# Reordering the first loads, and their PSUM banks, of an attention and feed-forward kernel

## The chip, the core and the metric

The kernel runs on one NeuronCore of a Trainium2 chip. The core has a tensor engine (PE, with its weight loads shown apart as PEld), a vector engine (DVE), an activation engine (ACT), a general engine (POOL) and a queue engine (SP), each with an instruction stream of its own; 16 DMA engines move data between HBM and the core's SBUF. PE writes into PSUM, eight banks of 128 partitions x 512 fp32. The metric is the device time of one execution in microseconds.

## The reference

Two parts, one after the other. First attention over a sliding window of 128 with a linear position bias (ALiBi): batch 8, 8 heads, sequence 576, head size 64. Then a feed-forward part over the 4608 tokens with an activation x * cos(x):

```
scores = q @ k.T / sqrt(64);  rel = pos_q - pos_k
scores = where(0 <= rel < 128, scores - slope[h] * |rel|, -1e9)
attn   = softmax(scores) @ v                     # (8, 8, 576, 64)
x      = attn.transpose(0, 2, 1, 3).reshape(4608, 512)
h      = x @ w_in                                # w_in  512 x 2048
out    = (h * cos(h)) @ w_out                    # w_out 2048 x 512
```

Inputs and output are fp32; the kernel computes its products in bf16.

## The kernel before

**Attention.** A batch's 576 queries are cut into blocks of 128 (the last has 64), and a block into units `(batch, block, half of the heads)`: the first and the last block are one unit each, blocks 1 to 3 two each, eight units per batch. A unit goes through: `scores` (products of k and q into two PSUM banks; for the first six units of batch 0 the bias is added by PE, by a product with the identity matrix, L583, ahead of the scores), `exps` (one exponential on ACT over both banks, L596), `mask` (a product on DVE with the exponential of the bias, L615, for all units whose bias was not added by PE), `pv` (product with V, whose 65th column gives the sum, L631 to L645), `norm` (reciprocal and scaling on DVE), and a transposition of the result into `xT`, by PE (`x_pe`) or by a DMA (`x_dma`). Which pair of banks a unit's scores use comes from `SLOT`: slot 0 is banks 4 and 5, slot 1 is 6 and 7, slot 2 is 2 and 3. Before the change the first seven units (phase -1) go in groups of two through slots 0 and 1, and their products with V into banks 2 and 3.

**Feed-forward.** Tokens go in nine chunks of 512. For each of 16 slices of 128 columns of w_in, `moe1` makes four matmuls (512 wide, L760), a sine on ACT (L765) and a product on DVE (L769); then `moe2` makes 64 matmuls with w_out (L813) for the chunk. In chunk 0 the first half of the slices is cut into narrower parts (`moe1_part`, L784), so that they can start as soon as some of the tokens are there. The units of later batches are worked between the matmuls of the chunks. ACT needs a table load to go from exponentials to sines and back.

**Loads.** q and k of batch 0 come in four pieces (`load_qk`, PIECES): piece 0 by SP and ACT, pieces 1 to 3 by POOL's queue; piece 2 ("the third piece", tokens 256 to 511) is the largest, piece 3 (qend, kend) the last 64 tokens. Then batch 1 in one piece each, into the same buffers `qB` as the pieces of batch 0, so that these loads wait until PE has transposed batch 0 out of them. V comes in five blocks of tokens per batch (`load_v`, L392), w_in in four parts (L424), w_out in four quarters (L431). All of these are issued by POOL in the order of the program. q and k are transposed by PE for batches 0 and 1 (`qk_transposes`, L510) and by DMA for the later ones.

**The order of the work.** The program lists operations with what they read and write; class `Plan` sorts them. It keeps a clock per engine, gives every operation an expected duration (`occ`) and an expected time until its result is there (`lat`), and takes, engine by engine, the operation that can start first, then by priority (`pri`) and by place in the list. For a load, `lat` is the time that the transfer keeps the DMA engines busy, summed up in the variable `wire`. POOL keeps the order of the list. The result is one fixed stream of instructions per engine, with waits on semaphores where one engine needs another's result: an engine does not pass a waiting instruction. So constants such as `lat` change no computation, but they change where in the stream each instruction stands. While PE has nothing to do at the start, the planner puts small matmuls on zeros (`filler`, L945) into its stream.

Of the kernel before, what the change touches and what calls it, by code (L numbers as in the profile page):

```python
# [286 lines left out]
def bass_alibi_sliding__then__act_gcu_kernel(  # L287
# [8 lines left out]
    with ExitStack() as ctx:  # L296
# [4 lines left out]
        op = R.op  # L301
# [34 lines left out]

        GROUPS = [[2] * 4] + [[3, 3, 2]] * 5 + [[3] * 3]
        SLOT = [4, 6, 2]
        QUOTA = [8, 8, 8, 8, 8, 8, 9]
        BIASED = [(0, 0, 0)] + [(0, qb, hh) for qb in range(1, 4) for hh in range(2)][:5]  # L340
        SB, UB, OB = [4, 5, 6, 7], [2, 3], [0, 1]
# [24 lines left out]
        def load_qk(which, src, b, n=0):  # L366
            t0, rr, _ = PIECES[b][n]
            c0 = 64 * (t0 // 32)
            rows = bass.AP(src.tensor, src[b].offset + 64 * t0,
                           [[64 * rr, 32], [64 * S, H], [1, 64 * rr]])  # L370
            if b == 0 and n == 0:
                op("sp" if which == "q" else "act", [lambda e: e.dma_start(qF[which][:, :, :], rows)],
                   w=[("qF", which)], dma=f"ld{which}f", occ=700 if which == "q" else 2000,
                   lat=4000 if which == "q" else 3300, pri=0)
                i = qF[which][:, :, :].rearrange("p y (j d) -> p y j d", j=4)
                o = qC[which][:, :, :, :].rearrange("p j y d -> p y j d")
                op(("act", "dve"),
                   {"act": lambda e: e.activation(o, i, ACTF.Copy),
                    "dve": lambda e: e.tensor_copy(o, i)},
                   r=[("qF", which)], w=piece_keys(which, b, n), occ={"act": 460, "dve": 330},  # L380
                   lat={"act": 560, "dve": 410}, pri=2)
                return
            o = qE[which][:, :, :] if t0 == 512 else qB[which][:, :, c0:c0 + 64 * rr]
            op("pool", [lambda e: e.dma_start(o, rows)],  # L384
               w=piece_keys(which, b, n), dma=f"ld{which}{n}", occ=750,
               lat={2: 600, 4: 800 if which == 'q' else 900,
                    8: 2600 if which == 'q' else 1300, 18: 2850}[rr])

        def load_v(b, order=range(NBLK), behind=()):
            for t in order:  # L390
# [32 lines left out]
        def load_w_in(f0, f1):  # L423
            op("pool", [lambda e: e.dma_start(  # L424
                w_in[:, :, 256 * f0:256 * f1],
                moe_w_in[:, 256 * f0:256 * f1].rearrange("(k p) c -> p k c", p=128))],
               w=[("wi", f) for f in range(f0, f1)], dma=f"wi{f0}", occ=750,
               lat=1300 * (f1 - f0))

        def load_w_out(u):  # L430
            op("pool", [lambda e: e.dma_start(  # L431
                w_out[:, 4 * u:4 * u + 4, :],
                moe_w_out[512 * u:512 * u + 512, :].rearrange("(f p) j -> p f j", p=128))],
               w=[("wo", u)], dma=f"wo{u}", occ=750, lat=2600)

        def constants():
            op("dve", lambda e: e.memset(zeros[:, :], 0.0), w=["zeros"], occ=60, pri=0)
# [109 lines left out]
        def t_first(u):  # L547
            return S * u[0] + 128 * u[1]

        def scores(us, slot):  # L550

            def f(e):
                ins = None
                for n, u in enumerate(us, slot):
                    b, qb, hh = u
                    banks = [SLOT[n], SLOT[n] + 1]
                    acc = u in BIASED
                    if qb == 0:
                        jobs = [(128 * pr, 128, pr, 0) for pr in range(NPAIR)]
                    elif qb == 4:  # L560
                        jobs = [(128 * pr + 64 * i, 64, pr, 3 + i) for pr in range(NPAIR)
                                for i in range(2)]
                    else:
                        jobs = [(256 * i + 128 * j, 128, 2 * hh + i, qb - 1 + j)
                                for i in range(2) for j in range(2)]
                    for n, (c0, n_, pr, kc) in enumerate(jobs):
                        stop = not acc or n == len(jobs) - 1
                        for x in range(2):
                            ins = e.matmul(ps[:, banks[x], c0:c0 + n_], keys_ap(b, x, pr, kc),  # L569
                                           query_ap(b, x, pr, qb, n_), start=not acc, stop=stop)  # L570
                return ins
            keys, held, occ = [], [], 0
            for n, u in enumerate(us, slot):
                keys += tkeys(u)
                held += [("B", SLOT[n] + x) for x in range(2)]
                occ += 250 if u[1] == 4 else 230
                if u in BIASED:
                    b, qb, hh = u
                    for x in range(2):
                        rhs = BT[:, x, :, 128:256] if qb == 0 else BT[:, x, 2 * hh:2 * hh + 2, :]  # L580
                        prs = range(NPAIR) if qb == 0 else range(2 * hh, 2 * hh + 2)
                        bank = SLOT[n] + x
                        op("pe", lambda e, rhs=rhs, bank=bank: e.matmul(  # L583
                            ps[:, bank, :], ident[:, :], rhs, start=True, stop=False),
                           r=[("BT", 2 * pr + x) for pr in prs] + ["ident"], w=[("B", bank)],
                           occ=216, lat=379, pri=2)
            op("pe", f, r=keys, w=held, occ=occ, lat=occ + 165, mode=1, pri=2)

        pcount = [0]
        pbuf = {}  # L590
# [1 line left out]
        def exps(u, n, table):  # L592
            banks = [SLOT[n], SLOT[n] + 1]
            i = pbuf[u] = pcount[0] % NP
# [235 lines left out]

        def attention(us, phase):

            begin, g = [], 0
            sizes = ([[2] * 4] + GROUPS + [[], []])[phase + 1]
            own = 3 in sizes
            for many in sizes:
                some = us[g:g + many]
                if phase < 0:
                    for n, u in enumerate(some):
                        scores([u], n)  # L840
                        exps(u, n, 0)
                        mask(u)
                        if us.index(u) == 1:
                            qk_transposes(0, "q", 2, [0], SB[2:4])
                else:
                    scores(some, 0)
                    for n, u in enumerate(some):
                        exps(u, n, 2 * phase + 2)
                if not own:
                    outs = [UB[0] if u[1] in (0, 4) else UB[n] for n, u in enumerate(some)]  # L850
                    for u in some if phase >= 0 else []:
                        mask(u)
                    sets = [list(zip(some, outs))]
                    if phase < 0 or any(u[1] in (0, 4) for u in some):
                        sets = [[x] for x in sets[0]]
                else:
                    sets = [[x] for x in zip(some, SLOT)]
                for set_ in sets:
                    if own:
                        mask(set_[0][0])  # L860
                    pv(set_)
                    after = []
                    for u, ub in set_:
                        n = ucount[0]
                        ucount[0] += 1
                        norm(u, ub, n)
                        soon = us.index(u) < (4 if phase else 2) and phase >= 0
                        after.append((soon, t_first(u) // CH > phase + 1, u, ub, n))
                    for soon, late, u, ub, n in after:
                        if soon:  # L870
                            begin.append(x_dma(u, n))
                        elif late:
                            x_dma(u, n)
                        else:
                            x_pe(u, ub, n)
                g += many
            return begin
# [3 lines left out]
        constants()  # L881
        load_qk("q", q, 0, 1)
        load_qk("k", k, 0, 1)
        load_v(0, [0])
        load_qk("q", q, 0, 2)
        load_qk("k", k, 0, 2)
        load_v(0, [1])
        load_w_in(0, 1)
        load_v(0, [2, 3])
        load_w_in(1, 2)  # L890
# [5 lines left out]
        for n in range(2):  # L896
            qk_transposes(0, "q", n, [0], OB[0:1])
            qk_transposes(0, "k", n, [0], OB[1:2])
        qk_transposes(0, "k", 2, [0], OB)
        every = [u for b in range(B) for u in units(b)]  # L900
        done = 7
        attention(every[0:done], -1)
# [9 lines left out]
        for c in range(NCH):  # L912
# [17 lines left out]
            n = QUOTA[c] if c < len(QUOTA) else 0  # L930
            begin = attention(every[done:done + n], c)
# [4 lines left out]
            while next_t < B and done >= 8 * (next_t - 1):  # L936
# [4 lines left out]
                if next_t < B:  # L941
# [2 lines left out]
            moe2(c)  # L944
        R.schedule(filler=lambda e: e.matmul(ps[:, UB[1], 0:128], zeros[:, :],  # L945
                                             zeros[:, :], start=True, stop=True),
                   fill=(900, 8300))
        R.emit(final=[f"st{i}" for i in range(NOB)])


# [26 lines left out]
```

## Time and profile before

| | us |
|---|---|
| median of 3 runs | 309.34 (309.11 to 309.6) |
| profiled execution | 309.74 |
| its span | 307.9 |
| PE busy | 299.7 |
| ACT busy | 199.9 |
| DVE busy | 194.1 |
| POOL busy | 97.0 |

The span runs from the first to the last instruction; 1.84 us of the profiled execution lie around it. Busy time is what an engine spends in instructions, so an engine's idle time is span less busy time. In a timeline a row gives start, duration, engine, line, operation, tiles and number of instructions, and in brackets the idle time in front of it with what ended it. The digits by slices are busy shares in tenths, each slice a fortieth of the span.

### The profile page before, as it was taken

The numbers are of one execution on the slowest core, as the hardware profiler recorded it, in microseconds if no ns is written. First come the engines' busy times: TensorE is split into PE (matmuls) and PEld (weight loads), VectorE is DVE, ScalarE is ACT, GpSimd is POOL, SyncE is SP. The second block draws the span as 40 slices with busy tenths as digits, with TensorE's granted clock in tenths as the row PEclk, the third lists the DMA queues.
The fourth block names the chain that finished last, engine by engine and source line by source line (L and its number), as shares of the span: only waits on it lengthen the run. The fifth ranks groups of instructions, "written<-read, shape, count | busy, mean of one in ns | idle before, by whom it ended". The sixth has DMA issues, their size and how long they took to land.

```text
span 307.9 us, 6411 instructions
## 1 busy us (share of the span) xinstructions
PE 299.7 (97%) x2556; PEld 157.4 (51%) x2600; DVE 194.1 (63%) x402; ACT 199.9 (65%) x268; POOL 97.0 (32%) x122
## 2 busy tenths in 40 slices
PE   8899999999999999999999999999999999999996
PEld 6685555445554555445544554455445554444444
DVE  6687777574668566856785568656966588742000
ACT  6888854885488746873688378746964588752211
POOL 8997201355055505550348023900500000000000
PEclk9999999999999999999999999999999999999999
DMA  9999999999399979999699959995991420001112
GB/s 148 173 204 207 207 162 203 140 162 181 105 127 130 170 122 141 129 168 106 155 122 156 151 109 150 165 179 96 169 106 44 113 70 0 0 0 70 68 73 97
DMA packets 150332, 39.08 MB, mean 127 GB/s; under 512 B 138912, under 2 KB 145312, under 8 KB 150304
## 3 DMA queue, kind: packets, MB, share of 16 engines
q0 software_dynamic: 100688, 18.10, 80.6%
q1 hardware_dynamic: 49344, 20.33, 33.2%
q8 instruction: 20, 0.33, 0.5%
q10 hardware_dynamic: 272, 0.26, 0.3%
q14 instruction: 8, 0.07, 0.1%
HBM read 36.70 MB, written 9.44 MB: 150 GB/s over the span
## 4 chain that ended last, share of the span: by engine, by line
PE 83%; DMA 7%; POOL 5%; ACT 2%; issue 1%; DVE 1%; POOLq 0%; ACTq 0%
PE ps L813 37%; PE ps L760 36%; DMA w_outb<-in_moe_w_out_dram 7%; PE ps L569 5%; ACT p L596 2%; PE ps L643 2%; PE ps L645 2%; POOL vp L392 1%; PE ps L631 1%; POOL w_inb L424 1%; POOL qrows L384 1%; POOL krows L384 1%; PE ps L635 1%; DVE p L615 1%; POOL w_outb L431 0%
## 5 line engine op out<-in xcount | busy, mean ns | idle before, releaser
L813 PE MATMUL ps<-w_outb,gT 128*128 128x512 bf16 (+2 forms) x566 | 132.8, 373 | 2.6 <-issue 1.1
L760 PE MATMUL ps<-xT,w_inb 128*128 128x512 bf16 x528 | 120.9, 379 | 0.9 <-issue 0.2
L769 DVE TENSOR_TENSOR gT<-ps,cos 128x512 bf16<-128x512 f32 x136 | 90.3, 688 | 21.1 <-ACT cos L765 16.3
L765 ACT ACTIVATE cos<-ps,halfpi 128x512 f32<-128x512 f32 x136 | 90.0, 688 | 18.9 <-PE ps L760 13.9
L596 ACT ACTIVATE p<-ps 128x1024 bf16<-128x1024 f32 x64 | 61.7, 1023 | 33.3 <-PE ps L569 33.3
L760 PEld LDWEIGHTS ps<-xT,w_inb 128*128 128x128 bf16 x544 | 52.0, 98 | 59.5 <-ACT p L596 0.6
L813 PEld LDWEIGHTS ps<-w_outb,gT 128*128 128x128 bf16 x592 | 53.2, 98 | 56.4 <-DMA w_outb<-in_moe_w_out_dram 1.7
L392 POOL DMA_DIRECT2D vp<-in_v_dram x40 | 33.7, 867 | 88.4 <-DMA xT<-xnat 68.9
L615 DVE TENSOR_TENSOR p<-p,emask 128x1024 bf16<-128x1024 bf16 x58 | 39.1, 682 | 26.8 <-ACT p L596 26.7
L820 ACT ACTIVATE ob<-ps 128x512 f32<-128x512 f32 (+2 forms) x21 | 12.1, 576 | 41.8 <-PE ps L813 35.3
L403 POOL DMA_DIRECT2D qnat<-in_q_dram x30 | 25.3, 876 | 23.1 <-DMA qt<-qnat 23.1
L403 POOL DMA_DIRECT2D knat<-in_k_dram x30 | 25.3, 874 | 11.1 <-DMA kt<-knat 8.3
L682 DVE TENSOR_TENSOR xnat<-ps,rec 128x256 bf16<-128x256 f32 x48 | 19.8, 420 | 1.3
L821 DVE COPY ob<-ps 128x512 f32<-128x512 f32 x16 | 10.9, 683 | 15.1 <-PE ps L813 15.1
L569 PE MATMUL ps<-qt,kt 64*128 64x128 bf16 (+1 forms) x576 | 19.4, 211 | 0.4 <-DVE qt L526 0.2
L569 PEld LDWEIGHTS ps<-qt,kt 64*128 64x128 bf16 x576 | 14.5, 94 | 9.7 <-issue 4.5
L643 PEld LDWEIGHTS ps<-vp,p 128*128 128x128 bf16 x192 | 14.2, 97 | 9.0 <-issue 6.1
L643 PE MATMUL ps<-vp,p 128*128 128x65 bf16 x192 | 17.4, 193 | 0.2 <-ACT xT L731 0.2
L645 PE MATMUL ps<-vp,p 128*128 128x65 bf16 x192 | 17.5, 193 | 0.0
L645 PEld LDWEIGHTS ps<-vp,p 128*128 128x128 bf16 x192 | 13.2, 97 | 2.3
L680 DVE RECIPROCAL rec<-ps 128x4 f32<-128x4 f32 x48 | 8.2, 176 | 6.3 <-PE ps L645 5.8
L631 PEld LDWEIGHTS ps<-vp,p 128*128 128x128 bf16 x128 | 7.3, 97 | 3.6 <-issue 1.8
(66 smaller groups left out, 150.0 us busy)
## 6 DMA issues: line engine op xcount, KB each, us to landing
out_dram<-ob SPq DMA_DIRECT2D x35, 256.0 KB, 2.2
vp<-in_v_dram POOLq DMA_DIRECT2D x32, 128.0 KB, 7.1
qnat<-in_q_dram POOLq DMA_DIRECT2D x24, 128.0 KB, 6.6
knat<-in_k_dram POOLq DMA_DIRECT2D x24, 128.0 KB, 5.1
w_outb<-in_moe_w_out_dram POOLq DMA_DIRECT2D x4, 512.0 KB, 21.9
w_inb<-in_moe_w_in_dram POOLq DMA_DIRECT2D x3, 512.0 KB, 12.8
qrows<-in_q_dram POOLq DMA_DIRECT2D x1, 576.0 KB, 15.6
krows<-in_k_dram POOLq DMA_DIRECT2D x1, 576.0 KB, 17.7
```

The lines of the kernel that those rows point to most:

```text
L392: op("pool", [lambda e, t=t, rows=rows: e.dma_start(vp[b % 2][0:rows, t, :, 0:64], v[b, :, 128 * t:128 * t + rows, :].rearrange("h p d -> ...
L403: fns.append(lambda e, t=t, rows=rows: e.dma_start(nat[which][0:rows, t, :, :], src[b, :, 128 * t:128 * t + rows, :].rearrange("h p d -> p ...
L569: ins = e.matmul(ps[:, banks[x], c0:c0 + n_], keys_ap(b, x, pr, kc), query_ap(b, x, pr, qb, n_), start=not acc, stop=stop)
L596: op("act", lambda e: e.activation(P[i][:, 0:1024], ps[:, banks[0]:banks[0] + 2, :].rearrange("p a b -> p (a b)"), ACTF.Exp, scale=0.125), ...
L615: op("dve", lambda e: e.tensor_tensor(p, p, m, ALU.mult), r=[("P", i), ("EM", 0), ("EM", 1)], w=[("P", i)], occ=600, lat=690, pri=1)
L643: e.matmul(o, P[i][:, c0:c0 + 128], V[:, qb - 1, h, 0:65], start=True, stop=False)
L645: ins = e.matmul(o, P[i][:, c0 + 128:c0 + 256], V[:, qb, h, 0:65], start=False, stop=True)
L682: op("dve", lambda e: e.tensor_tensor(o, U[:, :, :, 0:64], rv[:, :, :, None].broadcast_to([128, 2, 2, 64]), ALU.mult), r=[("rec", n % 4)], ...
L760: op("pe", lambda e, kc=kc: e.matmul(ps[:, bank, :], w_in[:, kc, 128 * fc:128 * fc + 128], xT[:, kc, r0:r0 + CH], start=(kc == 0), stop=(k ...
L765: op("act", lambda e: e.activation(cosb[ci][:, :], ps[:, bank, :], ACTF.Sin, bias=halfpi[:, 0:1]), r=["halfpi"], w=[("B", bank), ("cos", c ...
L769: op("dve", lambda e: e.tensor_tensor(gT[gi][:, fc, :], ps[:, bank, :], cosb[ci][:, :], ALU.mult), r=[("cos", ci)], w=[("B", bank)] + [("g ...
L813: op("pe", lambda e, t=t, fc=fc, bank=bank, j0=j0, j1=j1: e.matmul(ps[:, bank, 0:j1 - j0], gT[gi][:, fc, 128 * t:128 * t + 128], w_out[:, ...
```

## The change

V's first block goes behind the third pieces of q and k on POOL's queue, right in front of V's second block. Units 0 to 6 take their score banks from a list `FIRST` (slots 0, 1, 2, 0, 1, 0, 1), and their products with V go to the banks in `FIRST_PV` (0, 0, 2, 2, 3, 2, 3). The bias products of units 1 to 5 are listed as after the scores of unit 0. k's third piece is transposed after unit 2's scores, into banks 2 and 3, no longer ahead of all units into banks 0 and 1. Five of the planner's expected transfer times are lower, and the fillers end at 7.4 us of the planner's clock in place of 8.3. The planner makes all orders anew from this; `mask` itself is not edited, and its products move only as the planner moves them.

```diff
+        FIRST, FIRST_PV = [0, 1, 2, 0, 1, 0, 1], [0, 0, 2, 2, 3, 2, 3]
...
-               lat={2: 600, 4: 800 if which == 'q' else 900,
-                    8: 2600 if which == 'q' else 1300, 18: 2850}[rr])
+               lat={2: 370, 4: 800 if which == 'q' else 900,
+                    8: 1700 if which == 'q' else 1300, 18: 2790}[rr])
...
-               lat=1300 * (f1 - f0))
+               lat=1275 * (f1 - f0))
...
-               w=[("wo", u)], dma=f"wo{u}", occ=750, lat=2600)
+               w=[("wo", u)], dma=f"wo{u}", occ=750, lat=2540)
...
-        def scores(us, slot):
+        def scores(us, slot, after=()):
...
-                           occ=216, lat=379, pri=2)
-            op("pe", f, r=keys, w=held, occ=occ, lat=occ + 165, mode=1, pri=2)
+                           occ=216, lat=379, pri=2, after=after)
+            return op("pe", f, r=keys, w=held, occ=occ, lat=occ + 165, mode=1, pri=2)
...
-                    for n, u in enumerate(some):
-                        scores([u], n)
-                        exps(u, n, 0)
+                    for u in some:
+                        i = us.index(u)
+                        made.append(scores([u], FIRST[i], made[:1]))
+                        exps(u, FIRST[i], 0)
                         mask(u)
-                        if us.index(u) == 1:
+                        if i == 1:
                             qk_transposes(0, "q", 2, [0], SB[2:4])
+                        if i == 2:
+                            qk_transposes(0, "k", 2, [0], UB)
...
-                    outs = [UB[0] if u[1] in (0, 4) else UB[n] for n, u in enumerate(some)]
+                    outs = FIRST_PV[g:g + many] if phase < 0 else [UB[0] if u[1] in (0, 4) else UB[n] for n, u in enumerate(some)]
...
-        load_v(0, [0])
         load_qk("q", q, 0, 2)
         load_qk("k", k, 0, 2)
-        load_v(0, [1])
+        load_v(0, [0, 1])
...
-        qk_transposes(0, "k", 2, [0], OB)
...
-                   fill=(900, 8300))
+                   fill=(900, 7400))
```

In the streams as planned, PE's fillers go from 32 to 34 instructions; POOL has V's first block two places later; before the transposes of batch 1's q PE has 9 of the 512-wide matmuls of chunk 0 in place of 16, between those and the transposes of k 11 in place of 9, and behind these 12 in place of 7.

More of the change, by code (lines that the diff above doesn't have):

```diff
@@ L831, in attention @@
         def attention(us, phase):
-            begin, g = [], 0
+            begin, made, g = [], [], 0
             sizes = ([[2] * 4] + GROUPS + [[], []])[phase + 1]
```

## The prediction

> **What bounds the kernel now.** I read the page first, then the waits of the tensor engine (PE) in order of time, then busy time by stretches, then the DMA issues with their times to landing. The page:
>
> ```profile
> span 307.9 us, 6411 instructions
> PE 299.7 (97%) x2556; PEld 157.4 (51%) x2600; DVE 194.1 (63%) x402; ACT 199.9 (65%) x268; POOL 97.0 (32%) x122
> DMA  9999999999399979999699959995991420001112
> PE 83%; DMA 7%; POOL 5%; ACT 2%; issue 1%; DVE 1%; POOLq 0%; ACTq 0%
> q8 instruction: 20, 0.33, 0.5%
> ```
>
> PE is busy for 97% of the span, so only its 8.2 us of idle time or its order can give anything. The chain of waits starts on POOL, which issues the loads, and goes through the landing of w_out before PE takes it over. The DMA digits say that the 16 DMA engines are full from the first slices to about 90 us. So the edit, which lies within the first 50 us, must be read against landings. The timeline of PE's weight loads, which stand right in front of their matmuls, shows where it waits for them:
>
> ```profile
> 23.30 0.14 PEld L510 LDWEIGHTS ps<-ident,qend 128*64 128x64 bf16 x4 [0.22 <-DMA kend<-in_k_dram]
> ...
> 28.60 1.03 PEld L510 LDWEIGHTS ps<-ident,qrows 128*64 128x64 bf16 x36 [0.51 <-DMA qrows<-in_q_dram]
> ...
> 31.77 1.05 PEld L510 LDWEIGHTS ps<-ident,krows 128*64 128x64 bf16 x36 [0.42 <-DMA krows<-in_k_dram]
> ...
> 34.36 1.47 PEld L813 LDWEIGHTS ps<-w_outb,gT 128*128 128x128 bf16 x8 [0.25 <-DMA w_outb<-in_moe_w_out_dram]
> ...
> 39.44 0.55 PEld L813 LDWEIGHTS ps<-w_outb,gT 128*128 128x128 bf16 x4 [1.05 <-DMA w_outb<-in_moe_w_out_dram]
> ...
> 42.15 0.55 PEld L813 LDWEIGHTS ps<-w_outb,gT 128*128 128x128 bf16 x4 [0.36 <-DMA w_outb<-in_moe_w_out_dram]
> ```
>
> Six times between 23 and 42 us PE stands in front of a transfer: the last pieces of batch 0, q of batch 1, k of batch 1, then w_out's quarters. What PE saves before 23 us, it waits away here. By stretches (the bracketed number is instructions, the last three columns clock, DMA share, GB/s):
>
> ```profile
> 28.60:36.00 7.40, 7.19 (x94) 4.25 (x96) 6.70 (x11) 6.23 (x11) 2.04 (x3) 1.00 1.29 203
> 36.00:39.50 3.50, 2.85 (x35) 1.24 (x34) 1.57 (x4) 2.79 (x3) 0.00 (x0) 1.00 1.29 204
> 39.50:44.00 4.50, 4.34 (x60) 2.49 (x63) 2.66 (x8) 1.94 (x2) 0.00 (x0) 1.00 2.35 159
> 44.00:60.00 16.00, 15.84 (x149) 8.60 (x147) 10.96 (x28) 10.84 (x16) 4.19 (x5) 1.00 1.99 172
> 60.00:300.00 240.00, 237.52 (x1846) 118.42 (x1879) 152.08 (x300) 154.06 (x204) 62.98 (x75) 1.00 1.08 114
> ```
>
> From q's landing at 28.6 to 39.5 us PE idles 0.21 + 0.65 = 0.86 us. From 44 to 60 us it idles only 0.16 us, and over the 240 us after that 2.5 us, spread out: from w_out on, PE has no stall of any size left.
>
> **The change, step by step.** Three things move: the order of loads, the order of work on the start's banks, and, since the planner orders everything anew from its constants, PE's order up to 50 us.
>
> *The loads.* q's and k's third pieces go ahead of V's first block on POOL's queue. The same bytes are loaded and the same instructions issued. The issues and the matching landings:
>
> ```profile
> 2.20 0.72 POOL L384 DMA_DIRECT2D krows<-in_k_dram  x1
> 2.92 0.94 POOL L392 DMA_DIRECT2D vp<-in_v_dram  x1
> 3.85 0.70 POOL L384 DMA_DIRECT2D qrows<-in_q_dram  x1
> 4.54 0.72 POOL L384 DMA_DIRECT2D krows<-in_k_dram  x1
> ...
> 11.52 0.71 POOL L384 DMA_DIRECT2D kend<-in_k_dram  x1
> ...
> 12.98 0.70 POOL L384 DMA_DIRECT2D qrows<-in_q_dram  x1
> ```
> ```profile
> krows<-in_k_dram POOLq DMA_DIRECT2D x1, 128.0 KB, 3.9
> vp<-in_v_dram POOLq DMA_DIRECT2D x1, 128.0 KB, 4.1
> qrows<-in_q_dram POOLq DMA_DIRECT2D x1, 256.0 KB, 5.9
> krows<-in_k_dram POOLq DMA_DIRECT2D x1, 256.0 KB, 6.5
> ...
> kend<-in_k_dram POOLq DMA_DIRECT2D x1, 64.0 KB, 11.7
> ...
> qrows<-in_q_dram POOLq DMA_DIRECT2D x1, 576.0 KB, 15.6
> ```
>
> Issue plus time to landing gives k's second piece at 6.1 us, V's first block at 7.0, q's third piece at 9.75, k's third at 11.0, kend at 23.2, q of batch 1 at 28.6. The third pieces have equal size, yet q's needs 2.73 us behind V's block and k's 1.29 us behind q's: 1.44 us of excess that bytes do not explain. Two bounds for what the new order does to every later landing, as a shift s: if the excess belongs to the piece itself, s = 0; if it belongs to its place behind V's block, s = 1.44. A landing can also come later, since nothing excludes that V's block now takes up such an excess and adds to it; I put the lower end at -0.3. POOL does not set it: it issues q of batch 1 at 12.98 us, 15.6 us before it lands. That issue waits until PE has transposed the third pieces out of the same buffer; those transposes stay ahead of 12.5 us (below), so this stays hidden.
>
> The planner's constants in the diff go the same way: 900 ns less for q's third piece, 2 x 230 for the last pieces, 200 for eight w_in columns, 60 for q of batch 1: it plans with s = 1.62. That is a belief of the code, not a measurement, and I use it only as a neighbour of the upper bound.
>
> *Banks of the start.* Units 0, 1, 2 get pairs 4-5, 6-7, 2-3, so unit 2's scores need not wait for unit 0's exponential.
>
> ```profile
> 8.16 1.97 ACT L596 ACTIVATE p<-ps 128x1024 bf16<-128x1024 f32 x2
> 10.54 1.02 ACT L596 ACTIVATE p<-ps 128x1024 bf16<-128x1024 f32 x1 [0.40 <-PE ps L569]
> ...
> 13.70 2.11 ACT L596 ACTIVATE p<-ps 128x1024 bf16<-128x1024 f32 x2 [0.89 <-PE ps L569]
> 16.12 1.94 ACT L596 ACTIVATE p<-ps 128x1024 bf16<-128x1024 f32 x2 [0.31 <-PE ps L569]
> ```
>
> The third exponential can start at 10.13 instead of 10.54 us: 0.4 us. But k's third transposes now write banks 2-3 and wait for that exponential (ends 11.1), and on PE they queue behind unit 0's product with V, whose block lands last of the group, at about 11.0 us for s = 0. So they start near 11.2 us, as before (11.3), and unit 3 starts no more than 0.2 to 0.3 us earlier. Mask products: no line of `mask` changes; in the start only unit 6 has one, on DVE, which moves by a few places. All of this ends before the wait at 23.3 us and is worth nothing by itself while PE still waits there; where that wait is gone, it is worth its 0.2 to 0.3 us.
>
> *PE's order.* The planned orders set side by side show the part that counts. Before, 16 matmuls of the first product (512 wide, L760) stand between the partial products and the transposes of batch 1's q, 9 behind them, 7 behind k's. After: 9, 11 and 12. The transposes of the last pieces also come earlier, with 16 narrow and 16 middle matmuls behind them instead of 12 middle ones.
>
> ```profile
> 17.62 1.28 PE L784 MATMUL ps<-xT,w_inb 128*128 128x128 bf16 x20
> 23.65 1.48 PE L784 MATMUL ps<-xT,w_inb 128*128 128x256 bf16 x12
> ...
> 54.21 3.24 PE ps L760 x15
> ```
>
> So PE reaches the last pieces about 16 x 0.06 + 4 x 0.12 = 1.4 us earlier, at 21.7 us, and waits 1.5 us less s for kend at 23.2 - s. From there it has 0.3 + 1.0 + 2.0 + 9 x 0.216 = 5.2 us of work to the transposes of q, 28.5 - s, where q lands at 28.6 - s. Both landings give the same time, so this point is fixed by DMA and sits at 28.6 - s, as long as s is not over 1.5; past that PE's own work sets it. What is left behind it is before's work plus seven matmuls, 7 x 0.216 = 1.51 us. Against that, before's idle time behind this point is covered: at most 0.86 us; I take 0.8, since the switches between kinds of matmul remain. Net +0.7 us (bounds +0.65 and +1.1, the latter if only the 0.42 for k goes). Behind 44 us PE was dense before and stays so; the reshuffled orders of later chunks can move up to 0.3 us either way out of the 2.5 us, and I count 0.
>
> *Sum.* Time change = 0.7 - s. I take s = 1.4, the upper end, because the nearest row is k's third piece: same size, same form, directly behind a piece of its own kind, as q's will be. 0.7 - 1.4 = -0.7 us. The profiled execution took 309.74 us (span 307.9 and 1.84 around it), 0.4 above the median of 309.34; I apply the change to both: 309.04 for a profile, 308.6 us for the median.
>
> One rule speaks against this. The Trainium skill, "DMA: Bandwidth & Descriptors", section "Queues, rings and completion order", says that on each DMA engine the descriptors of a ring are consumed in ring order. By that rule a swap within one queue leaves everything behind the swapped group where it was, s = 0, and the sum would be +0.7 us. The trace agrees as to order (landings follow the issues), and cannot tell about the excess.
>
> **Rivals.** First: the excess stays, s = 0. PE then loses the seven matmuls at a wait it cannot pass: 309.34 + 0.7 = 310.0 us, slower. For it: no byte less is in front of batch 1's q; rates at 28 to 39 us are steady at 203 to 204 GB/s. Against it: 2.73 against 1.29 us. It decides as soon as s is below 0.1.
>
> Second: part of it goes. A transfer has landed when the last of 16 engines is done, and one late engine can be made late elsewhere, by the instruction loads on q8 (20 of 16 KB), for one. Then s is 0.1 to 1.3, say 0.7: 309.3 us, no change that can be told.
>
> Third: the start slips. If unit 0's product waits longer for V, k's third transposes and units 3 to 6 come later behind it on PE. It costs nothing up to the 1.5 us less s that PE waits at kend, and 1 us per us beyond: at s = 1.4 that cover is only 0.1 us plus the 0.2 gained on the start, so a slip of 0.9 us gives 308.6 + 0.6 = 309.2. For it: the product with V now stands in front of k's transposes on PE. Against it: V's block lands when the third exponential ends, for which those transposes wait anyway.
>
> **How the numbers follow.** s above 1.3 and no slip: 0.41, forecast 308.6 us, own range 308.1 to 308.9. Second rival 0.24 and third 0.09, together 0.33: 309.2 to 309.3, no change that can be told. First rival, s near 0 or below: 0.26, 310.0. What a measurement can tell from no change is 0.2%, 0.62 us: faster below 308.7, slower above 310.0. The range: downward s = 1.7 (the start's 0.2 us allow that) with 0.3 from later chunks and 0.1 of measurement, 309.34 + 0.7 - 1.7 - 0.4 = 307.9; upward s = 0 with 0.2 for the spread, 310.2.
>
> **What will show it.** Right: q's third piece lands less than 2 us behind k's second; q of batch 1 lands near 27.2 us and PE is there at that moment; w_out's third quarter is no longer waited for; after 45 us each product starts about 0.7 us earlier. Wrong: kend and q of batch 1 still land at 23.2 and 28.6 us, PE idles some 1.5 us before them, and w_out's products run 0.7 us later than before; or the landings come sooner and PE is not there yet, since units 3 to 6 are late.

## The result and the profile after

The changed kernel takes 310.35 us (median of 22 runs, 309.33 to 312.45) against 309.60 us of the kernel before on the same chips (22 runs): the ratio is 1.0024 (95% interval 1.0014 to 1.0034), 0.75 us slower. A second series gave 310.29 against 309.50 us, 1.0032 (1.0013 to 1.0050). The forecast was 308.6 us, faster; the outcome lies just outside its range, on the side of the rival that ends slower. Of the distance, 0.26 us is the kernel before itself, 309.60 us here against the 309.34 us from which the forecast started.

The execution that was profiled took 309.73 us, with a span of 307.9 us as before. It is one of the faster ones of this kernel, so its total tells nothing; its rows do. The page, with PE, the engines' share and the chain of waits:

```profile
span 307.9 us, 6416 instructions
PE 299.6 (97%) x2558; PEld 157.6 (51%) x2602; DVE 195.0 (63%) x403; ACT 200.0 (65%) x267; POOL 97.0 (31%) x122
...
PE 87%; DMA 4%; POOL 3%; ACT 3%; issue 1%; DVE 1%; ACTq 0%; POOLq 0%
```

DMA's share of the chain fell from 7 to 4%; the transfer in it is now kend, no longer w_out. The issues with their times to landing, to be set beside those of before (3.9 us for k's second piece, 5.9 for q's third, 11.7 for kend, 15.6 for q of batch 1):

```profile
qrows<-in_q_dram POOLq DMA_DIRECT2D x1, 256.0 KB, 5.2
...
krows<-in_k_dram POOLq DMA_DIRECT2D x1, 128.0 KB, 4.4
...
qrows<-in_q_dram POOLq DMA_DIRECT2D x1, 576.0 KB, 14.6
...
kend<-in_k_dram POOLq DMA_DIRECT2D x1, 64.0 KB, 11.2
```

By the trace's own times of issue and arrival q's third piece lands 1.46 us behind k's second one, kend at 22.62 (before 23.25), q of batch 1 at 27.48 (before 28.55). PE's waits in the stage, as the timeline of its weight loads shows them:

```profile
22.66 0.14 PEld L512 LDWEIGHTS ps<-ident,qend 128*64 128x64 bf16 x4 [1.27 <-DMA kend<-in_k_dram]
...
27.73 1.03 PEld L512 LDWEIGHTS ps<-ident,qrows 128*64 128x64 bf16 x36 [0.23 <-DMA qrows<-in_q_dram]
...
31.34 1.03 PEld L512 LDWEIGHTS ps<-ident,krows 128*64 128x64 bf16 x36 [0.42 <-issue]
...
35.83 0.64 PEld L815 LDWEIGHTS ps<-w_outb,gT 128*128 128x128 bf16 x4 [0.23 <-DMA w_outb<-in_moe_w_out_dram]
```

PE now stands 1.27 us in front of kend, reaches q of batch 1 when it lands, and waits for w_out only 0.23 us. But q's and k's transposes start 0.87 and 0.43 us sooner than before (28.60, 31.77), and w_out's wait at 35.83 is already behind a longer row of matmuls: what was gained at q is used up within 8 us. By stretches (length, then busy time of PE, PEld, DVE, ACT and POOL, clock, DMA share, GB/s):

```profile
27.70:36.00 8.30, 8.19 (x99) 4.71 (x101) 7.43 (x11) 7.44 (x12) 2.90 (x4) 1.00 1.27 201
36.00:39.50 3.50, 3.50 (x39) 1.67 (x38) 1.55 (x3) 3.24 (x4) 0.00 (x0) 1.00 1.28 204
39.50:44.00 4.50, 4.45 (x55) 2.52 (x54) 2.79 (x7) 1.96 (x3) 0.00 (x0) 1.00 2.38 157
```

From 36.0 to 39.5 us PE is busy for 3.50 of 3.50 us, where it was 2.85. Behind q of batch 1 this kernel is bound by PE alone.

### The profile page after: what moved, and what is told of

Its sections match the earlier page's. It is cut to its first block, busy times and chain, and to the rows that moved or that the text cites. A ratio compares the mean times of both kernels' runs of the same rounds, so it can differ in the third digit from the quotient of the medians.

```text
span 307.9 us, 6416 instructions
## 1 busy us (share of the span) xinstructions
PE 299.6 (97%) x2558; PEld 157.6 (51%) x2602; DVE 195.0 (63%) x403; ACT 200.0 (65%) x267; POOL 97.0 (31%) x122
## 4 chain that ended last, share of the span: by engine, by line
PE 87%; DMA 4%; POOL 3%; ACT 3%; issue 1%; DVE 1%; ACTq 0%; POOLq 0%
PE ps L762 38%; PE ps L815 37%; PE ps L571 5%; DMA kend<-in_k_dram 4%; ACT p L598 3%; PE ps L645 2%; PE ps L647 2%; PE ps L633 1%; POOL vp L394 1%; POOL w_inb L426 1%; DVE p L617 1%; PE ps L786 1%; PE ps L512 1%; PE ps L637 1%; POOL qrows L386 1%
## 5 line engine op out<-in xcount | busy, mean ns | idle before, releaser
L645 PEld LDWEIGHTS ps<-vp,p 128*128 128x128 bf16 x192 | 14.2, 97 | 10.0 <-issue 8.0
L647 PEld LDWEIGHTS ps<-vp,p 128*128 128x128 bf16 x192 | 13.2, 97 | 2.0
```

What stands on the lines that cost most here:

```text
L645: e.matmul(o, P[i][:, c0:c0 + 128], V[:, qb - 1, h, 0:65], start=True, stop=False)
L647: ins = e.matmul(o, P[i][:, c0 + 128:c0 + 256], V[:, qb, h, 0:65], start=False, stop=True)
```

## The experiments

Two things were moved, the landings and PE's order, and the first four runs take them apart: the five constants alone, the changed kernel without them, its banks alone, its loads alone. Of after_3, before_2, after_4 and e_after_gap_2 there is one execution each, with its profile.

### PE's order alone: the five constants in the kernel before

```diff
-               lat={2: 600, 4: 800 if which == 'q' else 900,
-                    8: 2600 if which == 'q' else 1300, 18: 2850}[rr])
+               lat={2: 370, 4: 800 if which == 'q' else 900,
+                    8: 1700 if which == 'q' else 1300, 18: 2790}[rr])
...
-               lat=1300 * (f1 - f0))
+               lat=1275 * (f1 - f0))
...
-               w=[("wo", u)], dma=f"wo{u}", occ=750, lat=2600)
+               w=[("wo", u)], dma=f"wo{u}", occ=750, lat=2540)
```

> The kernel before with the five new transfer constants alone: loads and banks as before, but the planner now puts 10 of the 512-wide matmuls ahead of the transposes of batch 1's q (before 16), 11 behind them (9) and 11 behind k's (7). Theory A (the loss is PE's order: matmuls moved behind a landing that does not move): 6 x 0.216 - 0.8 = +0.5 us, range +0.2 to +0.9, with over 1 us of idle time at kend and q together. Theory B (the loss is the start's banks or loads): within 0.2 us of before.

Measured: 309.98 against 309.53 us, ratio 1.0013 (1.0003 to 1.0023). No load and no bank has moved; q of batch 1 lands at 28.35 us. The planner puts 10, 11 and 11 of the 512-wide matmuls around the transposes of q and k (before 16, 9, 7). The timeline of PE's weight loads in this kernel:

```profile
23.12 0.14 PEld L510 LDWEIGHTS ps<-ident,qend 128*64 128x64 bf16 x4 [1.09 <-DMA kend<-in_k_dram]
...
28.40 1.03 PEld L510 LDWEIGHTS ps<-ident,qrows 128*64 128x64 bf16 x36 [0.42 <-DMA qrows<-in_q_dram]
```

PE gets to kend early and stands there for 1.09 us in place of 0.22. So an order that expects landings sooner than they come costs 0.45 us by itself, against +0.5 us by theory A.

### The changed kernel with the old constants

The same three edits the other way round, in the changed kernel.

> The changed kernel with the five old transfer constants: loads and banks as changed, but 15 matmuls ahead of the transposes of batch 1's q, 11 behind them, 6 behind k's. Theory A: the loss goes and what the loads give stays: 0 to -1.0 us against before, by how much sooner q of batch 1 and w_out land in it. Theory B: as slow as the changed kernel, +0.7 us.

Measured: 309.41 us, ratio 1.0000 (0.9989 to 1.0011). The loss is gone, and so it sits in the order that the constants make; of the gain of up to 1.0 us that was expected with it, nothing shows. q of batch 1 lands at 27.19 us and kend at 21.49 in its profile, the soonest of all profiles, and this brings nothing. The timeline of PE's weight loads says why:

```profile
23.02 0.14 PEld L512 LDWEIGHTS ps<-ident,qend 128*64 128x64 bf16 x4
...
28.49 1.03 PEld L512 LDWEIGHTS ps<-ident,qrows 128*64 128x64 bf16 x36 [0.42 <-issue]
```

No landing is waited for, and PE still comes to q at 28.49 us (28.60 and 28.50 in the two profiles of before). With 15 matmuls in front of q, PE's own work ends where the landing used to be. In the kernel before, the two limits lay on top of each other.

### The banks alone

The changed kernel with the old constants and the old order of loads.

```diff
+        load_v(0, [0])
         load_qk("q", q, 0, 2)
         load_qk("k", k, 0, 2)
-        load_v(0, [0, 1])
+        load_v(0, [1])
```

> Banks, transposes and fillers as changed; loads and constants as before. 17, 8 and 7 matmuls around the transposes, so nearly before's order there. Theory A: the start is 0.2 to 0.7 us sooner and waits it away at kend and q, within 0.3 us of before. Theory B: +0.7 us.

Measured: 309.76 us, ratio 1.0009 (0.9998 to 1.0020): nothing that can be told, as the prediction had it. kend is waited for 0.58 us, so what PE saves on the start it waits away there.

### The order of loads alone

```diff
-        load_v(0, [0])
         load_qk("q", q, 0, 2)
         load_qk("k", k, 0, 2)
-        load_v(0, [1])
+        load_v(0, [0, 1])
```

> The loads' order alone: V's first block behind the third pieces, all else and the constants as before. 12, 9 and 11 matmuls around the transposes. If the excess of q's third piece belongs to its place behind V's block, that piece lands under 2 us behind k's second and q of batch 1 lands near 27.5 us; if it belongs to the piece, 28.5 us. Time by theory A: 4 x 0.216 - 0.8 - s, so 0 to -0.9 us. A rival by which the loads' order itself costs time, since unit 0's product waits for V's block: +0.3 to +0.7 us.

Measured: 309.56 us, ratio 1.0009 (0.9989 to 1.0029). kend lands at 22.68, q of batch 1 at 27.90 us, 0.57 and 0.65 us sooner than in the profile of before, and the time is the same, where 0 to 0.9 us less were expected. PE comes to q later than the landing, as in the run above:

```profile
28.63 1.03 PEld L510 LDWEIGHTS ps<-ident,qrows 128*64 128x64 bf16 x36 [0.42 <-issue]
```

### One constant

```diff
-               lat={2: 370, 4: 800 if which == 'q' else 900,
+               lat={2: 900, 4: 800 if which == 'q' else 900,
```

In the changed kernel this alone lets the planner set the last pieces' transposes behind all but 4 of the 13 parts of chunk 0's partial products (8 of them stood behind), and 14, 11 and 7 matmuls around those of q and k.

> The changed kernel with one constant moved: the last pieces' transfer time 900 in place of 370. The planner then puts all but 4 of the 13 parts ahead of their transposes (before 3 behind, changed 8 behind) and 14, 11 and 7 matmuls around those of batch 1's q and k in place of 9, 11 and 12. Loads, banks and the other four constants stay as changed. Theory A: the loss goes, 309.0 to 309.6 us, with under 0.5 us of idle time at kend and q. If the loss came from the other constants, the banks or the loads: 310.3 us.

> The changed kernel once more, for a second profile and beside the next run. By theory A (PE's order stands too early for the landings) its time hangs on when kend and q of batch 1 land: 309.7 to 310.4 us against 309.5 for before, with 1 to 2 us of idle time of PE at kend and q together; kend between 22.0 and 23.2 us, q of batch 1 between 27.2 and 28.2. If the loss were elsewhere, two executions with different landings would not differ in the time at which w_out's products start.

> The kernel before once more, for a second profile of its landings: q's third piece 2.5 to 3.5 us behind V's first block and q of batch 1 at 28.2 to 28.8 us, if the three profiles with the old order of loads tell a rule; under 28.0 us if the difference of 1 us to the three with the new order is chance.

> The changed kernel a third time, one look: as for the second, and q of batch 1 under 28.0 us if the new order of loads brings landings forward as a rule.

Measured side by side: 309.38 us, ratio 1.0001 (0.9986 to 1.0016), beside 1.0032 (1.0013 to 1.0050) for the changed kernel as it is (after_2); the single executions took 309.31 us (before_2) and 309.89 us (after_3). With four parts more in front of kend and five matmuls more in front of q's landing, the whole loss is gone. The waits of e_lastlate, first the timeline of PE's weight loads, then the sums of waits from 44 to 60 us:

```profile
22.74 0.14 PEld L512 LDWEIGHTS ps<-ident,qend 128*64 128x64 bf16 x4
...
27.99 1.03 PEld L512 LDWEIGHTS ps<-ident,qrows 128*64 128x64 bf16 x36 [0.42 <-issue]
```
```profile
PEld ps L762 <- DMA xT<-xfirst: 0.9, 1, 0.9
```

No landing is waited for at kend or at q (q landed at 27.48, PE comes at 27.99). Further on it meets a new one: the first 128 rows of batch 1 of x, transposed by a DMA that SP issues at 45.3 us, 0.9 us at about 54 us.

The profiles before_2 and after_3 hold all matmul records (x2600 and x2602; the profile of before had x2556), so that PE's stretch behind q of batch 1 can be measured in full. From the start of q's transposes to DVE's first product of chunk 1 (length, PE, clock, DMA share, GB/s), before_2, after_3 and then the first profile of before:

```profile
28.50:55.83 27.33, 26.98 (x317) 1.00 1.76 190
```
```profile
27.72:56.27 28.55, 28.54 (x323) 1.00 1.75 178
```
```profile
28.60:56.22 27.62, 26.49 (x311) 1.00 1.75 187
```

Before: 27.33 us with 0.35 us idle. After: 28.55 us with 0.01 idle. The stretch is 1.22 us longer: the seven matmuls (1.51 us) less 0.35 us of idle time, to 0.06 us. In the first profile of before, which lacks matmul records, the same stretch is 27.62 us long, so against it the changed kernel's is 0.93 us longer; its idle time, with the busy time of before_2, would be about 0.64 us (an estimate). The same sum for e_lastlate, from 27.99 to 55.78 us, gives 27.79 us with 0.44 us idle.

### Is the gain eaten by x's transfer?

The four kernels here are e_lastlate again, and three kernels (e_lastlate, the changed one, the one before) in which PE, and not SP's DMA, transposes the first rows of batch 1 of x:

```diff
-                        soon = us.index(u) < (4 if phase else 2) and phase >= 0
+                        soon = us.index(u) < (4 if phase else 1) and phase >= 0
```

> The changed kernel with the one constant of the last pieces set late, once more, as the base for the next three. Its first profile showed PE waiting 0.9 us at 54 us for the transposed copy of x that SP issues at 45.3 us (xfirst, landed 8.7 us later), and no wait of over 0.35 us on a load between 20 and 44 us. Both theories expect 309.4 us again, ratio to before 0.9990 to 1.0010, and that wait between 0.3 and 1.0 us.

> The same, but the first 128 rows of batch 1 of x are transposed by PE, with two copies, instead of by SP's DMA. Theory A, that the sooner landings are lost again because the next thing PE meets is this DMA copy of x at 54 us: the wait of 0.9 us goes, PE pays four transposes (0.24 us), so about -0.6 us against the base, 308.8 us, ratio to before 0.998. Theory B, that PE is held behind 24 us by its own work and by banks, and the wait for x only shows idle time that stands elsewhere otherwise: no gain, 309.4 to 309.6 us.

> The changed kernel with the first 128 rows of batch 1 of x transposed by PE. Two later profiles of the changed kernel showed a wait of 0.4 us on that copy. Theory A: -0.4 + 0.24, about -0.2 us, 310.1 us, still slower than before by 0.5 us, since the seven matmuls behind q's landing stay. Theory B: no gain or +0.2 us, 310.3 to 310.5 us.

> The kernel before with the same edit of x alone. Its profile shows no wait on that copy (issued at 45.4 us, 6.9 us to landing at the most, first use at 54.0 us). Theory A: only the price of four transposes, +0.2 us, 309.7 us. If it gains as much as the others do, the edit is worth something for another reason and A is not shown by it.

Measured: 309.35 us (ratio 0.9992, 0.9980 to 1.0004) for the base, again with the wait of 0.9 us; 311.08 (1.0051, 1.0035 to 1.0068), 311.92 (1.0077, 1.0052 to 1.0102) and 310.53 us (1.0036, 1.0023 to 1.0049) for the three with the edit. Both theories missed: the edit costs 1.0 us in the kernel before, where nothing was to be saved, and 1.6 to 1.7 us in the others. So this is no way to take that wait away. The 0.9 us are the wait of a weight load, of which 0.27 us stand at the same place in before_2 with no landing to wait for; PE itself idles 0.44 us there in e_lastlate (0.40 in e_lastlate_2), which is all of its idle time from q's transposes to chunk 1. So the wait can be worth some 0.4 to 0.6 us at most, an estimate from these rows. That it exists is shown, that it eats the gain is not.

### Does q's third piece hold up k's second one?

The profiles so far showed something else: k's second piece, in front of the moved one on the queue, lands 3.9 to 4.7 us behind its issue in the five profiles with the old order of loads and 4.4 to 6.0 us in nine with the new one. To see whether the closeness of the next issue does it, POOL got two index fills of a scratch tile between the two issues, which move q's third piece and all later issues by 0.76 us and leave PE's order as it was:

```diff
         load_qk("k", k, 0, 1)
+        for _ in range(2):
+            op("pool", lambda e: e.iota(gap[:, :, :], pattern=[[128, 2], [-1, 128]], base=-128,
+                                        channel_multiplier=1,
+                                        allow_small_or_imprecise_dtypes=True),
+               w=["gap"], occ=1, lat=340)
         load_qk("q", q, 0, 2)
```

> The changed kernel, with two index fills of a scratch tile on POOL (together about 1.0 us) between the issue of k's second piece and that of q's third: every later issue is 1 us later, PE's order and the load order stay. Theory C, q's third piece right behind k's second delays the landing of that one: k's second piece lands 3.9 to 4.5 us behind its issue again, the first scores' exponential starts near 7.5 us instead of 7.8 to 8.8, and the time falls by 0.3 to 0.5 us to 309.8 to 310.0 us; kend then lands as late as with the old order. Theory D, the spread of that landing is chance and has nothing to do with what stands behind it: 4.4 to 6.0 us again, and no change in time, 310.3 us.

> The same gap in the changed kernel with the one constant set late. Theory C: k's second piece 3.9 to 4.5 us behind its issue, time 309.0 us, 0.4 us below the 309.4 us without the gap. Theory D: 309.4 us.

> The changed kernel once more, for the spread of one landing: Theory C expects k's second piece 4.4 to 6.0 us behind its issue; theory D the same.

> The changed kernel with the gap once more, for the spread of one landing: theory C expects k's second piece 3.9 to 4.5 us behind its issue, theory D 4.4 to 6.0 us.

Measured: 310.46 us (1.0046, 1.0028 to 1.0064) for the changed kernel with the gap and 309.63 us (1.0006, 0.9996 to 1.0016) for e_lastlate with it, and 311.01 and 311.21 us in the single executions of e_after_gap_2 and after_4; k's second piece lands 3.9, 5.3 and 5.0 us behind its issue with the gap, 5.7 in after_4, the changed kernel once more. The gap brings no time, against theory C; one landing in three is as early as in the old order, so it does not decide on the landing either. What makes that piece late in the new order is open.

The first of these runs is useful in another way. In its profile q of batch 1 lands where it did in the kernel before, at 28.51 us, though the rest is the changed kernel:

```profile
23.47 0.14 PEld L513 LDWEIGHTS ps<-ident,qend 128*64 128x64 bf16 x4 [1.67 <-DMA kend<-in_k_dram]
...
28.55 1.03 PEld L513 LDWEIGHTS ps<-ident,qrows 128*64 128x64 bf16 x36 [0.24 <-DMA qrows<-in_q_dram]
```

Its span is 308.8 us, against 307.9 in the profile of before with the same landing: the price of PE's order with nothing gained on the loads, 0.9 us.

The run after_4 shows how the start can go wrong. Timeline of PE's weight loads, then the windows of after_4, then the same window of the kernel before (columns as above: length, PE, PEld, DVE, ACT, POOL, clock, DMA share, GB/s):

```profile
7.95 0.40 PEld L512 LDWEIGHTS ps<-ident,krows 128*64 128x64 bf16 x8 [1.80 <-DMA krows<-in_k_dram]
```
```profile
8.00:11.30 3.30, 3.30 (x35) 1.74 (x35) 0.69 (x1) 1.62 (x2) 3.30 (x5) 0.52 1.82 167
11.30:20.00 8.70, 8.43 (x158) 5.87 (x155) 5.64 (x19) 7.22 (x10) 7.65 (x12) 1.00 1.53 194
```
```profile
8.00:11.30 3.30, 2.82 (x56) 1.83 (x51) 1.78 (x5) 2.90 (x4) 3.30 (x5) 1.00 1.49 164
```

PE waits 1.80 us for k's second piece, and then runs for 3.3 us at a granted clock of 0.52: 35 matmuls where the kernel before does 56. The first exponential starts at 9.60 us (8.16 before), PE comes to kend after it has landed, and the whole kernel is late: span 309.4 us. The landing alone does not make this: in after_2 k's second piece lands only 0.13 us sooner (7.78 us against 7.91), PE waits 1.10 us and goes on at a clock of 1.00, and its first exponential starts at 8.83 us, 0.77 us sooner.

## Why the prediction was wrong

The changed kernel's profiles side by side; landings are issue plus time to landing in the trace, the last column is span less landing of q of batch 1:

| profile | k's 2nd piece, us behind issue | first exponential | wait at kend | q of batch 1 lands | span | difference |
|---|---|---|---|---|---|---|
| before | 3.9 | 8.16 | 0.22 | 28.55 | 307.9 | 279.3 |
| before_2 | 4.2 | 7.49 | 0.21 | 28.19 | 307.5 | 279.3 |
| after | 4.4 | 7.79 | 1.27 | 27.48 | 307.9 | 280.4 |
| after_3 | 5.0 | 8.22 | 0.57 | 27.68 | 308.1 | 280.4 |
| after_2 | 5.6 | 8.83 | 0.21 | 27.95 | 308.4 | 280.4 |
| e_after_gap | 3.9 | 8.20 | 1.67 | 28.51 | 308.8 | 280.3 |
| after_4 | 5.7 | 9.60 | none | 27.70 | 309.4 | 281.7 |

Four executions of the changed order agree to 0.1 us: span is q's landing plus 280.4 us; before it was plus 279.3. So the form of the prediction's sum, a price of PE's order minus s, is what happens, as long as PE gets to q in time. Both terms were mis-sized. (e_after_gap_2 is left out of the table: there w_out is late as well, 1.6 us of waits for it, span 309.2.)

**The term that failed: s = 1.4.** I took the upper bound because k's third piece, directly behind a piece of its own kind, was the nearest row. The third piece did behave like that row: 1.46 us behind the piece before it, in place of 2.73 behind V's block. But a shorter distance on the queue is not a shift of everything behind. Over all profiles (five with the old order of loads, ten with the new one, those with the gap left out) kend lands at 23.27 and 22.40 us on the mean, q of batch 1 at 28.50 and 27.71: s = 0.8 to 0.9, with single values from 27.19 to 28.24 us for q. And k's second piece, which no step of the prediction looks at, lands at 6.47 and 7.31 us, 0.84 us later. On the mean the three swapped pieces land within 3.59 us behind it in place of 4.82, 1.23 us less, but since it is later itself, the last of them is only 0.39 us sooner (10.90 us against 11.29). What makes it later is not shown. The second rival (a part of it goes, s about 0.7) had the size right and the time wrong, since it took over the other term.

The Trainium skill, "DMA: Bandwidth & Descriptors", section "Queues, rings and completion order", had descriptors consumed in ring order on each engine, from which I made s = 0. The trace marks the arrival of each of the 16 shares of a transfer: the first share of q of batch 1 comes at 26.23 us with the old order and 25.86 with the new one, the last at 28.50 and 27.71. So about 0.4 us is a sooner first share and 0.4 us a smaller lag of the last one. The measurement lies between what I made of the rule and my bound.

**The other term: +0.7 for PE's order.** The mechanism was right: PE stands at kend 1.27 us (forecast 1.5 less s), reaches q with its landing, and has seven matmuls left behind it. The price was not 0.7 but 0.9 to 1.2 us, about its own upper bound. The failed step is "at most 0.86 us of idle time, I take 0.8": of the 1.51 us only 0.3 to 0.6 us were covered. The 0.42 us in front of k's transposes stays in every profile, now as issue time of PE, and the profile with all records has only 0.35 us of idle time behind q. Part of the 0.86 was matmuls missing from the profile of before: between q's and k's transposes it has 8 of the 9 matmuls and puts 0.16 us of idle time in the place of the ninth.

**The sum.** 1.1 - 0.8 = +0.3 us for executions whose start is in time; measured were +0.75 and +0.79 between the medians. By the line of the table, 310.3 us (span 308.5) is a landing near 28.1 us, so the common execution gains less than the profiled ones do, or starts late; with four profiles of the changed kernel neither is shown.

**The third rival, the start slips.** It happens, though at k's second piece and not at V's block. It costs nothing while PE waits at kend, as the rival said: the first exponential moves from 7.79 to 8.83 us and the wait at kend falls from 1.27 to 0.21, with the span still on the line. Beyond that cover it is paid: after_4 is 1.3 us off the line, most of it by the lower clock behind the wait. Such a drop shows in an execution's mean clock, 0.994 or 0.995, in three of the 34 executions of the two series of the changed kernel; without them their medians are still 310.33 and 310.22 us. How much of the 0.75 us smaller slips make is not measured, since only profiled executions show them.

**The banks.** Right: the third exponential no longer waits, sine's table is loaded at 17.41 us in place of 18.08, and alone it changes nothing (1.0009, 0.9998 to 1.0020).

**Behind 44 us, 0 +- 0.3.** Right for the later chunks: from chunk 1's first product to the last one it takes 222.44 us in both profiles of before and 222.50 to 222.59 in three of the changed kernel. The wait of 0.4 us for x's DMA copy at 54 us, in after_2 and after_3, was not foreseen; it is a wait of a weight load, of which 0.27 us stand at the same place in before_2, and PE itself idles only 0.01 us in the stretch that holds it.

**First rival, s = 0, 310.0 us, slower.** It came nearest in time, for a reason that is half its own: s was not 0, but PE's order cost more. That its number came nearest is in part luck.

**What this makes of the change.** In the kernel before, PE came to q's transposes as q landed, busy up to there but for 0.22 us at kend and some 0.1 us at q, and had 0.35 us of idle time behind them (some 0.6 in the first profile). Sooner landings under the old order find PE busy (28.49 and 28.63 us in e_oldconsts and e_loads), and an order that is there sooner has moved the same work behind q, where nearly nothing is idle to take it. So neither half can win more than those tenths, and the two together lose what the landings fall short of the order: 1.1 against 0.8. That was in reach of the prediction: the trace of before held both limits at one place. Of the signs named for a right forecast the landings came (1.46 us; q at 27.48 us with PE there), and the time did not: DVE's first product of chunk 1 starts at 56.18 us, before at 56.23. The prediction's reading that the DMA engines are full to about 90 us is also off: the digit of the eleventh slice, 77 to 85 us, is 3; nothing in the sum rests on it.

Not settled are why k's second piece lands later, how often the start slips without a drop of the clock in executions without a profile, and how much of the 0.4 to 0.6 us the wait for x in e_lastlate is worth.

## What to carry to other kernels

Where an engine reaches a landing just as it comes, a sooner landing is worth only the idle time around that point, however far it moves: sum that idle time first. Work that a planner moves to the other side of a landing costs its full length unless idle time stands there. When a transfer lands sooner because its neighbour on the queue changed, look at the piece in front as well as at the ones behind, and at the spread over several executions; and idle time read as a difference of busy times is only as good as the count of records beside it.

## What was not expected of the hardware

The granted clock falls in the middle of the start. Where PE waits 1.80 us (after_4) or 2.1 us (e_after_xpe) for k's second piece, it runs at about 0.5 for some 3 us afterwards; at a wait of 1.7 us (e_lastlate_xpe) or 1.10 us (after_2) it stays at 1.00. The mean clock of an execution tells it: 0.994 or 0.995 in 8 of 96 executions of kernels with the new order of loads and no gap, in none of 24 with the gap, and never below 0.999 in 132 with the old order. The Trainium skill, "TensorE: Matmul & The Clock Gate", section "Part 1: The HAM clock gate (the "warmup" mystery)", gives an idle window of about 3.4 us for that; here a gap of 1.8 us, with PE busy on both sides, was enough. By the clock's own records in the trace the drop lasts 3.41 us in both, and in the 3.41 us ahead of it PE is busy 1.76 us (after_4) and 1.43 us (e_after_xpe); e_lastlate_xpe, busy 1.88 us of the 3.41 us that hold its wait, keeps 1.00. Three executions do not make this a threshold.

The last of the 16 shares of kend and of q of batch 1 lags the first by 1.2 to 2.8 us, and this lag alone differs by up to 0.7 us between two executions of the same kernel (2.73 us in before and 2.03 in before_2 for q of batch 1; in after and after_2 its first share comes at 25.78 us and the last at 27.48 and 27.95).
